# Retention and two feed-forward layers on one core: keeping a second token block in SBUF, splitting inputs earlier, starting the last phase's copies later

## The chip, the cores and the metric

The kernel runs on 1 core of one Trainium2 chip. The metric is the device time of one execution in microseconds (us): 1074.28 us before the change, the median of 3 runs (1074.26 to 1076.01).

## The reference, cut to what matters

Four sequences of 768 tokens with 8 heads of 64 go through a retention layer (a decaying linear attention), and its output, as 3072 rows of 512, through two feed-forward layers of width 2048.

```python
for t in range(S):
    state = gamma[None, :, None, None] * state + np.einsum('bhd,bhe->bhde', k[:, :, t], v[:, :, t])
    y[:, :, t] = scale * np.einsum('bhd,bhde->bhe', q[:, :, t], state)
...
x = np.ascontiguousarray(attn_out.transpose(0, 2, 1, 3)).reshape(B * S, H * D)
h = x @ w_in;  g = np.maximum(0.01 * h, h);               x = g @ w_out     # first layer
h = x @ w_in2; g = h * (1.0 / (1.0 + np.exp(-1.702 * h))); y = g @ w_out2   # second layer
```

## The kernel before, in words

All is computed in float32. A product of two float32 matrices is made of three matmuls on parts: every operand is split into a high part (a rounded copy, made by ScalarE) and a low part (the operand less its high part, a subtraction on VectorE or GpSimd), and high x low, high x high and low x high are added up in PSUM. The weights arrive as float64 words and are turned into float32 in the kernel. The engines' queues are written out by hand: the order of the calls in the code is the order on each engine, and every engine and every queue of transfers takes its instructions strictly in that order. `later.at(n, ...)` puts a step n turns later; a turn is one `later.tick()`, once per tile of the first layer.

**Retention** (`retention`) goes in 24 steps `s`, each a chunk of 128 tokens, 6 chunks a sequence. Tokens are grouped in 6 blocks of 512, so steps 0 to 3 are block 0, steps 4 to 7 block 1. In a step, in this order:

- TensorE makes the scores of chunk s+1 (L277), VectorE masks them (L280);
- from step 4 on a piece n of the first layer's weights is converted (`work_first`): two ScalarE instructions (L172, L173), then four on VectorE (L176, L178, L180, L182), which need the first of ScalarE's;
- TensorE makes the chunk's output: the state's addition (L300, not in the last chunk of a sequence), then L307 and L313, which need the state that VectorE left at L316;
- `a_store` scales the output out of PSUM (VectorE). For block 0 this takes three instructions (L329, which put the two halves of every second head pair in place), then a rounded copy on ScalarE (L338) and the subtraction on GpSimd, so that both parts stay in SBUF, ready as operands. For all other blocks it takes one instruction (L341) and, every second chunk, three transfers into a scratch tensor `xd0[blk]` in HBM (`swapped`, L161 and L163);
- `work_last`: weights piece n-1 is split (ScalarE L154, GpSimd L151) and piece n rounded (L191, on GpSimd for the first two pieces);
- ScalarE scales the keys of chunk s+2 by their decay (L288, 8 instructions);
- SyncE (SP) issues the load of chunk s+4 (L267);
- from step 6 on `ffn_in(0, m)`: one tile of the first layer's first product for block 0, 12 matmuls (L238), and its eviction by ScalarE (L242). Its third matmul needs the low part of weights piece m from GpSimd.

**The first layer's first product for blocks 1 to 5** follows: for each block 16 tiles `m` of 12 matmuls, PSUM in 6 banks, evicted in turn by ScalarE (L242). Beside it ScalarE and VectorE prepare the other weights (`Prep`, 9 pieces a block): a load, conversion three turns later (L172 to L191 and sums), a split one turn after that for some, and a store by SP six turns after the load, in a ring of three places (areas b, b and c). The conversion writes into a place from which the store of three pieces before must have been read.

A block's input comes back from HBM with `x_load` (L205, one transfer of 1 MB on SP's queue into the single buffer `x_raw`) and is split in four quarters with `x_split`, each a ScalarE copy (L154) and a VectorE subtraction (L151). The last quarter's `x_split` also issues the `x_load` of the block after it, which must wait until that quarter has been read. Split inputs lie in two areas in turn: "d" for even blocks, "a" for odd ones.

**The other phases** (L770 and L581 on TensorE) are the remaining three products in Strassen form. The last one (`second2`) is begun in the third's piece 26 by `second2.begin`: its loads at once, and its first four high and low parts (L727 on ScalarE, L151 on VectorE) from 14 turns later on.

Of the kernel before, what the change touches and what calls it, by code (L numbers as in the profile page):

```python
# [24 lines left out]
NP = H // 2  # L25
NC = S // P
KF = DFF // P
TB = 512
NB = NT // TB
CPB = TB // P  # L30
N_STEPS = B * NC

NQ = KF // 2
# [54 lines left out]
def retention_two_ffn(ctx: ExitStack, tc: tile.TileContext, qkv, consts, small, w1i, w1o, w2i, w2o, scratch, out):  # L88
# [30 lines left out]
    def areas(tags, dt=F32):  # L119
        return [Area(t, dt) for t in tags]  # L120
# [9 lines left out]
    later2 = Later()  # L130
# [6 lines left out]

    xs_a = areas("da", F32R)
    xs = [[xs_a[u].view(4 * k, 2, TB) for k in range(NP)] for u in range(2)]
    x0 = xs_a[0].view(0, NP, 2, TB)  # L140
    x_raw = Area("c1").view(0, NP, TB)
    g_area = Area("e")
    g_ring = ring(run_of(g_area, 6, 2), TB)
# [6 lines left out]
    def subtract(o, x, y, e=nc.vector):  # L150
        e.tensor_tensor(out=o, in0=x, in1=y, op=ALU.subtract)  # L151

    def split(hi, lo, src, eng=nc.vector):
        nc.scalar.copy(out=hi, in_=src)  # L154
        subtract(lo, src, hi.bitcast(F32), eng)
# [3 lines left out]
    def swapped(d, s):  # L159

        nc.sync.dma_start(out=d[:, 0::2], in_=s[:, 0::2])  # L161
        for r, t in halves:
            nc.sync.dma_start(out=d[r, 1::2], in_=s[t, 1::2])  # L163

    def load_raw(m):
        raw[m] = t = next(raw_ring).bitcast(U32)
        nc.sync.dma_start(out=t, in_=w1i[m].bitcast(U32).rearrange("p (f two) -> p f two", two=2))
# [36 lines left out]
    def x_load(q):  # L204
        nc.sync.dma_start(out=x_raw, in_=xd0[q])  # L205

    def x_split(q, k):
        split(xs[q % 2][k][:, 0], xs[q % 2][k][:, 1], x_raw[:, k])
        if k == NP - 1 and q + 1 < NB:
            x_load(q + 1)  # L210
# [5 lines left out]
    def work_first(n):  # L216
        if n + 2 < KF:
            load_raw(n + 2)
        if n < KF:
            convert(n)  # L220

    def work_last(n):
        if 0 < n <= KF:
            finish(n - 1)
        if n < KF:
            round_up(*conv[n], nc.gpsimd if n < 2 else nc.vector)
# [19 lines left out]
    def retention():  # L246
# [11 lines left out]
        steps = [(b, c) for b in range(B) for c in range(NC)]  # L258
# [4 lines left out]
        def a_load(s):  # L263
            ins[s] = next(in_ring)
            n = 2 if s < 3 else 4
            for i in range(0, 4, n):
                nc.sync.dma_start(out=ins[s][:, i : i + n], in_=qkv[s, :, i : i + n])  # L267

        def a_scores(s):
            t = ins[s]  # L270
            qT = t[:, 0].rearrange("p (n i) -> p n i", n=NP)
            kT = t[:, 1].rearrange("p (n i) -> p n i", n=NP)
            ps = banks[:, 0:2].rearrange("p e (n i) -> p e n i", n=NP)
            for n in range(NP):
                for e in range(2):
                    r = slice(D * e, D * e + D)
                    nc.tensor.matmul(out=ps[:, e, n], lhsT=kT[r, n], rhs=qT[r, n], start=True, stop=True,  # L277
                                     skip_group_check=True)
            sm = next(sm_ring)
            nc.vector.tensor_tensor(out=sm, in0=ps, in1=mask, op=ALU.mult)  # L280
            sc_t[s] = sm

        def a_decay(s):
            b, c = steps[s]
            if c < NC - 1:
                ks_t[s] = ins[s][:, 2].rearrange("p (h d) -> p h d", h=H)
                for h in range(H):
                    nc.scalar.activation(out=ks_t[s][:, h], in_=ks_t[s][:, h], func=AF.Copy, scale=kdec[:, c, h : h + 1])  # L288
# [31 lines left out]
        def a_store(s, o):  # L320
            blk, cc = divmod(s, CPB)
            cols = slice(cc * P, cc * P + P)
            if cc % 2 == 0:
                a_store.x = next(x_ring)
            x = a_store.x[:, :, cc % 2 * P : cc % 2 * P + P]

            def put(r, u, t):
                n = 2 * P
                nc.vector.tensor_tensor(out=x[r].rearrange("p (m u) i -> p u m i", u=2)[:, u],  # L329
                                        in0=o[t, u, :n].rearrange("p (m i) -> p m i", i=P),  # L330
                                        in1=qdec[t].rearrange("p (m u) i -> p u m i", u=2)[:, u], op=ALU.mult)

            if blk == 0:
                put(slice(0, P), 0, slice(0, P))
                for r, t in halves:
                    put(r, 1, t)

                nc.scalar.copy(out=x0[:, :, 0, cols], in_=x)  # L338
                subtract(x0[:, :, 1, cols], x, x0[:, :, 0, cols].bitcast(F32), nc.gpsimd)
                return  # L340
            nc.vector.tensor_tensor(out=x.rearrange("p (m u) i -> p u m i", u=2),  # L341
                                    in0=o[:, :, : 2 * P].rearrange("p u (m i) -> p u m i", i=P),
                                    in1=qdec.rearrange("p (m u) i -> p u m i", u=2), op=ALU.mult)
            if cc % 2:
                swapped(xd0[blk][:, :, cc * P - P : cc * P + P], a_store.x)
            if s == 2 * CPB + 1:
                x_load(1)

        ins[0] = next(in_ring)
        nc.scalar.dma_start(out=smalls, in_=small)  # L350
# [16 lines left out]
        def keep_warm(n):  # L367

            for _ in range(n):
                nc.tensor.matmul(out=warm, lhsT=idle[:, :P], rhs=idle, start=True, stop=True, skip_group_check=True)  # L370
# [5 lines left out]
        for s in range(len(steps)):  # L376
            if s == 0:
                keep_warm(6)
            elif s + 1 < len(steps):
                a_scores(s + 1)  # L380
            n = None
            if s >= W0 - 2 and done[0] < KF + 1 and (s <= W0 or now_in[s - 1]):
                n = done[0]
                done[0] += 1
                work_first(n)
            o = a_out(s)
            a_store(s, o)
            if n is not None:
                work_last(n)
            if s == 0:  # L390
                a_scores(1)
                keep_warm(6)
            if s + 2 < len(steps):
                a_decay(s + 2)
            if s + 4 < len(steps):
                a_load(s + 4)
            if s in (1, 2):
                load_raw(s - 1)
            if s >= len(steps) - 4:
                x_split(1, s - len(steps) + 4)  # L400
            for m in now_in[s]:
                ffn_in(0, m)

# [95 lines left out]
    def w_split(q, a, b):  # L499
        for hi, lo in w_parts(q, a, b):  # L500
            split(hi.bitcast(F32R), lo.bitcast(F32R), lo)
# [351 lines left out]


    retention()

    h_banks[:] = range(6)
# [14 lines left out]
    for blk in range(1, NB):  # L872
        for m in range(KF):
            n = (blk - 1) * KF + m
            if given < min(N_IN1, (n + 1) * N_IN1 // 64):
                Prep(*names[given], prep_rings).start(later)
                given += 1
            if blk + 1 < NB:
                if m in (8, 9, 10, 11):
                    x_split(blk + 1, m - 8)  # L880
            elif m == 11:
                second1.begin(later, 2 * NQ, 2 * NQ, 3, 1)
            ffn_in(blk, m, second1.place(0, 1, *divmod(m, NQ)) if blk + 1 == NB else None)
            if blk + 1 == NB and m in freed:
                q = freed[m]
                for a, b in ((3, 7), (0, 3)) if m < 11 else ((6, 7), (3, 6), (0, 3)):
                    w_load("1o", q, a, b)
                if m < 11:
                    later.at(3, lambda q=q: w_split(q, 3, 7))
                    later.at(4, lambda q=q: w_split(q, 0, 3))  # L890
            later.tick()
# [14 lines left out]
    def done1(n, blk, i, q):  # L906
# [19 lines left out]
        if i == 2 and q < 3:  # L926
# [8 lines left out]
    second2 = Second({"x": run_of(x_a, 8, 2), "y": run_of(y_a, 8, 2), "z": run_of(z_a, 8, 2),  # L935
                      "ops": run_of(o_a[0], 4, 4) + run_of(o_a[1], 1, 4),
                      "u": run_of(u_a[0], 2, 4) + run_of(u_a[1], 2, 4)},
                     gd2, {"d": (4, 5), "e": (6, 7), "f": (0, 1), "h": (2, 3)})
# [7 lines left out]
    def step2(n):  # L946
        if n < 5:
            w_load("2i", n + 3, 0, 7)
        if 1 <= n <= 5:
            behind.extend(w_steps(n + 2, 3, 7) + w_steps(n + 2, 0, 3))  # L950
        if n in (4, 5):
            todo[n - 4].load()
        if n == 5:
            waiting.extend(todo[2:])
        if 6 <= n < 24 and n % NQ in range(1, 7) and todo:
            p = todo.pop(0)
            behind.extend([lambda: behind.extendleft(reversed(p.steps() + [lambda: p.finish(later2, waiting)]))])
        if n == 26:
            second2.begin(later2, 0, NQ, 4, 14)

    def done2(blk, q):
        if blk < 3:
# [146 lines left out]
```

## Time and profile before

| | |
|---|---|
| median of 3 runs | 1074.28 us (1074.26 to 1076.01) |
| the profiled execution | 1073.59 us |
| its span in the trace | 1071.5 us |
| TensorE (PE) busy | 1052.3 us, 98% |
| VectorE (DVE) busy | 816.0 us, 76% |
| ScalarE (ACT) busy | 585.4 us, 55% |
| GpSimd (POOL) busy | 93.3 us, 9% |

The profiled execution lasts 2.1 us longer than its span and 0.69 us less than the median. Busy shares are means over phases; matmuls overlap, so a busy PE is not PE at its peak. Where PE loses time is read from single stretches.

### The profile page before, as it was taken

The numbers are of one execution on the slowest core, as the hardware profiler recorded it, in microseconds if no ns is written. First come the engines' busy times: TensorE is split into PE (matmuls) and PEld (weight loads), VectorE is DVE, ScalarE is ACT, GpSimd is POOL, SyncE is SP. The second block draws the span as 40 slices with busy tenths as digits, with TensorE's granted clock in tenths as the row PEclk, the third lists the DMA queues.
The fourth block names the chain that finished last, engine by engine and source line by source line (L and its number), as shares of the span: only waits on it lengthen the run. The fifth ranks groups of instructions, "written<-read, shape, count | busy, mean of one in ns | idle before, by whom it ended". The sixth has DMA issues, their size and how long they took to land.

```text
span 1071.5 us, 16963 instructions
## 1 busy us (share of the span) xinstructions
PE 1052.3 (98%) x6042; PEld 902.4 (84%) x6043; DVE 816.0 (76%) x1380; ACT 585.4 (55%) x1116; POOL 93.3 (9%) x91
## 2 busy tenths in 40 slices
PE   8999999999899999999999999999999999999998
PEld 6777788887688888888888999999999788888886
DVE  5988737977796698787788767676867995885883
ACT  5866435645464554544545666465666555555553
POOL 2312100000000000000000104434300000000000
PEclk9999999999999999999999999999999999999999
DMA  9999665998896523525437936648387535335322
GB/s 342 348 396 337 213 228 188 314 316 302 294 350 227 172 80 128 187 79 177 138 123 280 354 121 228 222 157 307 122 316 257 183 99 197 102 96 197 107 70 79
DMA packets 128164, 225.81 MB, mean 211 GB/s; under 512 B 11088, under 2 KB 72784, under 8 KB 124752
## 3 DMA queue, kind: packets, MB, share of 16 engines
q1 hardware_dynamic: 97440, 178.29, 48.7%
q10 hardware_dynamic: 30640, 46.45, 11.7%
q8 instruction: 47, 0.77, 0.3%
q14 instruction: 37, 0.30, 0.1%
HBM read 138.71 MB, written 85.98 MB: 210 GB/s over the span
## 4 chain that ended last, share of the span: by engine, by line
PE 78%; DVE 8%; DMA 8%; ACT 3%; issue 2%; ACTq 0%; SPq 0%; DVEq 0%
PE psum L770 40%; PE psum L581 21%; PE psum L238 12%; DMA h<-qkv 2%; PE psum L277 1%; DMA b<-w1o 1%; PE psum L307 1%; DMA b<-gd 1%; DVE b L151 1%; PE psum L994 1%; DMA wd1o<-b 1%; DVE b L191 1%; DMA xd<-h 1%; PE psum L300 1%; DMA gd<-e 1%
## 5 line engine op out<-in xcount | busy, mean ns | idle before, releaser
L770 PE MATMUL psum<-c,h 128*128 128x512 f32 x1008 | 228.8, 389 | 0.0
L770 PEld LDWEIGHTS psum<-c,h 128*128 128x128 f32 x1008 | 189.2, 188 | 39.3
L770 PE MATMUL psum<-e,h 128*128 128x512 f32 x768 | 182.1, 391 | 1.0 <-DVE e L151 1.0
L770 PEld LDWEIGHTS psum<-e,h 128*128 128x128 f32 x768 | 143.3, 188 | 31.6 <-DVE e L151 1.3
L238 PE MATMUL psum<-d,h 128*128 128x512 f32 x576 | 138.2, 397 | 4.9 <-DVE d L151 3.3
L238 PEld LDWEIGHTS psum<-d,h 128*128 128x128 f32 x576 | 107.8, 190 | 31.1 <-DVE d L151 3.7
L238 PE MATMUL psum<-a,h 128*128 128x512 f32 x576 | 131.5, 389 | 0.0
L238 PEld LDWEIGHTS psum<-a,h 128*128 128x128 f32 x576 | 107.9, 188 | 23.0 <-ACT e L242 0.4
L581 PE MATMUL psum<-b,h 128*128 128x384 f32 x576 | 110.4, 334 | 2.1 <-ACT psum L654 2.1
L581 PE MATMUL psum<-c,h 128*128 128x384 f32 x576 | 110.1, 334 | 0.3 <-DVE d L618 0.3
L581 PEld LDWEIGHTS psum<-b,h 128*128 128x128 f32 x576 | 100.7, 188 | 2.8 <-ACT psum L654 2.8
L581 PEld LDWEIGHTS psum<-c,h 128*128 128x128 f32 x576 | 100.7, 188 | 0.6 <-DVE d L618 0.6
L727 ACT CAST c<-b 128x512 fp32r<-128x512 f32 x96 | 59.2, 622 | 57.1 <-DVE c L151 35.6
L601 ACT ACTIVATE d<-psum 128x384 f32<-128x384 f32 x96 | 47.1, 492 | 65.0 <-PE psum L581 54.8
L151 DVE TENSOR_TENSOR c<-b,c 128x512 fp32r<-128x512 f32 x96 | 65.4, 689 | 18.8 <-ACT c L727 16.6
L242 ACT ACTIVATE e<-psum 128x512 f32<-128x512 f32 x80 | 47.3, 591 | 42.7 <-PE psum L238 37.6
L727 ACT CAST e<-a 128x512 fp32r<-128x512 f32 x77 | 47.3, 622 | 41.6 <-PE psum L770 17.1
L151 DVE TENSOR_TENSOR h<-h 128x384 fp32r<-128x384 f32 (+2 forms) x80 | 44.9, 595 | 31.9 <-ACT h L154 20.4
L151 DVE TENSOR_TENSOR e<-a,e 128x512 fp32r<-128x512 f32 x77 | 52.3, 688 | 18.5 <-ACT e L727 17.1
L151 POOL TENSOR_TENSOR a<-a 128x768 f32<-128x768 f32 x7 | 13.2, 1891 | 509.4 <-DMA h<-wds 461.4
L605 DVE TENSOR_TENSOR d<-psum,d 128x384 f32<-128x384 f32 x96 | 52.1, 549 | 4.3 <-ACT d L601 3.6
L770 PE MATMUL psum<-f,h 128*128 128x512 f32 x192 | 49.0, 390 | 0.0
(148 smaller groups left out, 1469.6 us busy)
## 6 DMA issues: line engine op xcount, KB each, us to landing
gd<-d ACTq DMA_DIRECT2D x128, 192.0 KB, 3.6
h<-qkv SPq DMA_DIRECT2D x21, 1024.0 KB, 8.6
gd<-e ACTq DMA_DIRECT2D x80, 256.0 KB, 5.0
d<-gd SPq DMA_DIRECT2D x64, 256.0 KB, 3.8
b<-gd SPq DMA_DIRECT2D x64, 256.0 KB, 4.0
a<-gd SPq DMA_DIRECT2D x48, 256.0 KB, 5.1
c<-w1i SPq DMA_DIRECT2D x16, 512.0 KB, 7.7
xd<-e SPq DMA_DIRECT2D x12, 512.0 KB, 3.2
```

The lines of the kernel that those rows point to most:

```text
L151: e.tensor_tensor(out=o, in0=x, in1=y, op=ALU.subtract)
L191: e.tensor_tensor(out=f.bitcast(I32), in0=f.bitcast(I32), in1=low.bitcast(I32), op=ALU.add)
L238: nc.tensor.matmul(out=h, lhsT=w[:, a, k], rhs=xs[blk % 2][k][:, c], start=(i == 0), stop=(i == 3 * NP - 1), skip_group_check=True)
L242: nc.scalar.activation(out=t, in_=h, func=AF.Lrelu)
L277: nc.tensor.matmul(out=ps[:, e, n], lhsT=kT[r, n], rhs=qT[r, n], start=True, stop=True, skip_group_check=True)
L300: nc.tensor.matmul(out=kv[r, n], lhsT=ks[:, 2 * n + e], rhs=v[:, n, r], start=(c == 0 and n == 0), stop=True, skip_group_check=True)
L307: nc.tensor.matmul(out=out(n, e), lhsT=v[:, n, r], rhs=sm[:, e, n], start=(n < 2), stop=(c == 0), skip_group_check=True)
L581: nc.tensor.matmul(out=t, lhsT=w[:, k, a], rhs=x[:, b, k], start=(start and m == 0), stop=(m == 5), skip_group_check=True)
L601: nc.scalar.activation(out=s, in_=src, func=AF.Sigmoid, scale=1.702)
L605: nc.vector.tensor_tensor(out=dst, in0=src, in1=s, op=ALU.mult)
L727: nc.scalar.copy(out=t[:, 0], in_=self.block_of(*item))
L770: nc.tensor.matmul(out=t[:, j], lhsT=w[:, j, a], rhs=x[:, b], start=(new and q == 0 and m == 0), stop=(q == NQ - 1 and m == 2), skip_group ...
```

## The change

Three edits. Block 1's retention result now stays in SBUF like block 0's (`blk < 2`), in area "a", so the scratch tensor `xd0[1]`, its load and its `x_split` go; the load of block 2 is issued in step 13. The `x_split` of the next block is called at tiles 2, 4, 6 and 8 instead of 8, 9, 10 and 11. The last phase's first parts are made 22 turns after `second2.begin` instead of 14.

```diff
@@ -137,7 +137,7 @@
     xs = [[xs_a[u].view(4 * k, 2, TB) for k in range(NP)] for u in range(2)]
-    x0 = xs_a[0].view(0, NP, 2, TB)
+    x_first = [t.view(0, NP, 2, TB) for t in xs_a]
@@ -330,7 +330,8 @@
-            if blk == 0:
+            if blk < 2:
+                x0 = x_first[blk]
                 put(slice(0, P), 0, slice(0, P))
                 for r, t in halves:
                     put(r, 1, t)
@@ -343,8 +344,8 @@
-            if s == 2 * CPB + 1:
-                x_load(1)
+            if s == 3 * CPB + 1:
+                x_load(2)
@@ -396,8 +397,6 @@
-            if s >= len(steps) - 4:
-                x_split(1, s - len(steps) + 4)
@@ -876,8 +875,8 @@
             if blk + 1 < NB:
-                if m in (8, 9, 10, 11):
-                    x_split(blk + 1, m - 8)
+                if m in (2, 4, 6, 8):
+                    x_split(blk + 1, m // 2 - 1)
@@ -956,7 +955,7 @@
-            second2.begin(later2, 0, NQ, 4, 14)
+            second2.begin(later2, 0, NQ, 4, 22)
```

Two places show what stands where. ScalarE's queue in steps 4 and 5 of retention, before (L172 and L173 convert a weights piece, L154 splits the one before it, L288 decays the keys; h_84 is the area of the retention chunks, h_412 that of the weights):

```order
L172 ACTIVATE b<-c_233 128x512
L173 ACTIVATE c_233<-c_233 128x512
L288 ACTIVATE h_84<-h_84,f 128x64 x8
L172 ACTIVATE b<-c_233 128x512
L173 ACTIVATE c_233<-c_233 128x512
L154 CAST h_412<-b 128x512
L288 ACTIVATE h_84<-h_84,f 128x64 x8
```

and now, where L339 is the rounded copy that was L338 before (the weights' area is now h_417):

```order
L172 ACTIVATE b<-c_233 128x512
L173 ACTIVATE c_233<-c_233 128x512
L339 CAST a<-h_84 128x4x128
L288 ACTIVATE h_84<-h_84,f 128x64 x8
L172 ACTIVATE b<-c_233 128x512
L173 ACTIVATE c_233<-c_233 128x512
L339 CAST a<-h_84 128x4x128
L154 CAST h_417<-b 128x512
L288 ACTIVATE h_84<-h_84,f 128x64 x8
```

In each of steps 4 to 7 a copy of the chunk's output now stands between the conversion of a weights piece and all that follows on ScalarE; on GpSimd its subtraction likewise stands ahead of the weights piece's.

SP's queue late in block 3, before (L205 is the load of block 5's input, L420 loads of weights, L455 and L456 stores of prepared ones from areas e, f, b and c):

```order
L420 DMA b<-w2i 128x2x256 x2
L455 DMA wds<-e 128x896
L456 DMA wds<-b 128x896
L420 DMA c_1600<-w2i 128x2x256 x2
L205 DMA c_81<-xd_5_71 128x2048
L455 DMA wds<-f 128x896
L456 DMA wds<-c_1600 128x896
```

and now, with every line number below the retention one less:

```order
L419 DMA b<-w2i 128x2x256 x2
L205 DMA c_81<-xd_5_71 128x2048
L454 DMA wds<-e 128x896
L455 DMA wds<-b 128x896
L419 DMA c_1605<-w2i 128x2x256 x2
L454 DMA wds<-f 128x896
L455 DMA wds<-c_1605 128x896
```

The input's load has moved three tiles forward, ahead of one weights load and one pair of stores; it stands in the same way in blocks 1 and 2.

## Rows read from the trace of the kernel before

**Rows 1.** Windows of 20 us: busy time by engine, TensorE clock, DMA share, GB/s
```profile
40.00:60.00 20.00, 20.00 (x237) 15.95 (x235) 18.94 (x28) 13.61 (x38) 5.17 (x4) 1.00 1.02 371
```
**Rows 2.** Chain that ended last, in order of time, blocks 1 to 5: start, length
```profile
134.12 16.56 PE psum L238 x72
...
283.17 76.45 PE psum L238 x336
```
**Rows 3.** Timeline where block 4 begins: start, length, instruction, [idle before <-what ended it]
```profile
266.53 2.34 PE L238 MATMUL psum<-d,h 128*128 128x512 f32 x9 [1.33 <-ACT e L242]
...
272.15 0.33 SPq L205 DMA_DIRECT2D c<-xd  x1
272.18 10.76 PE L238 MATMUL psum<-d,h 128*128 128x512 f32 x39 [3.31 <-DVE d L151]
...
273.01 0.42 SPq L456 DMA_DIRECT2D wds<-c  x1
...
281.40 0.66 ACT L172 ACTIVATE c<-c 128x512 f32<-128x512 f32 x1 [6.21 <-DMA gd<-e]
```
**Rows 4.** Window of 2 us in the same stretch
```profile
274.00:276.00 2.00, 2.00 (x6) 1.53 (x5) 1.79 (x4) 0.73 (x2) 0.00 (x0) 0.50 0.88 303
```
**Rows 5.** Timeline of SP and of ScalarE at the end of block 2
```profile
218.53 0.34 SPq L205 DMA_DIRECT2D c<-xd  x1
...
226.28 0.66 ACT L172 ACTIVATE c<-c 128x512 f32<-128x512 f32 x1 [8.00 <-DMA b<-w1o]
```
**Rows 6.** Timeline of ScalarE in steps 2 to 8 of retention
```profile
20.27 0.62 ACT L338 CAST d<-h 128x512 fp32r<-128x512 f32 x1 [0.64 <-DVE h L329]
20.80 2.01 ACT L288 ACTIVATE h<-h,f 128x64 f32<-128x64 f32 x8
...
24.22 0.69 ACT L172 ACTIVATE b<-c 128x512 f32<-128x512 f32 x1
...
36.48 1.28 ACT L242 ACT_TABLE_LOAD   x1
...
42.93 0.57 ACT L242 ACTIVATE e<-psum 128x512 f32<-128x512 f32 x1
...
43.96 0.70 ACT L172 ACTIVATE b<-c 128x512 f32<-128x512 f32 x1 [0.46 <-ACT e L242]
```
**Rows 7.** Timeline of VectorE in the same steps
```profile
18.94 1.29 DVE L329 TENSOR_TENSOR h<-psum,f 128x256 f32<-128x256 f32 x3 [0.30 <-PE psum L313]
...
24.94 1.02 DVE L176 TENSOR_SCALAR c<-c 128x512 uint32<-128x512 uint32 x1
...
27.39 0.42 DVE L316 TENSOR_TENSOR b<-psum,f 128x256 f32<-128x256 f32 x1
27.73 0.68 DVE L341 TENSOR_TENSOR h<-psum,f 128x512 f32<-128x512 f32 x1
...
39.64 0.42 DVE L176 TENSOR_SCALAR c<-c 128x512 uint32<-128x512 uint32 x1
```
**Rows 8.** Timeline of GpSimd in step 2
```profile
20.97 1.27 POOL L151 TENSOR_TENSOR d<-h,d 128x512 fp32r<-128x512 f32 x1 [1.91 <-ACT d L338]
```
**Rows 9.** Timeline of TensorE in steps 6 to 9
```profile
33.33 3.02 PE L238 MATMUL psum<-d,h 128*128 128x512 f32 x12
...
39.62 3.01 PE L238 MATMUL psum<-d,h 128*128 128x512 f32 x12
...
45.75 3.04 PE L238 MATMUL psum<-d,h 128*128 128x512 f32 x12
...
49.80 0.69 PE L300 MATMUL psum<-h 128*64 128x64 f32 x16
```
**Rows 10.** Timeline of TensorE in step 12
```profile
67.30 1.16 PE L277 MATMUL psum<-h 64*128 64x128 f32 x16 [0.54 <-DMA h<-qkv]
```
**Rows 11.** Timeline of ScalarE and TensorE in the third product, behind `second2.begin`
```profile
793.42 0.62 ACT L504 CAST h<-h 128x512 fp32r<-128x512 f32 x1 [3.08 <-DMA h<-wd2o]
...
795.38 2.37 PE L581 MATMUL psum<-b,h 128*128 128x384 f32 x12 [1.47 <-ACT psum L654]
```

## The prediction

> **What bounds the kernel now.** I read the busy shares first: TensorE 98% of the span. Then the chain that ended last, to see whether any other engine holds a long piece of it: it runs through TensorE's product L238 for hundreds of matmuls at a time [rows 2]. Then windows, which say where the remaining 2% lie. Even in retention, where the change works, TensorE is busy for 20.00 of 20.00 us while transfers move 371 GB/s [rows 1]. So shorter work elsewhere gains nothing by itself; a gain must remove a wait of TensorE, and a loss is a new wait of TensorE that nothing behind it gives back, since all behind it is TensorE's own work. Last I read timelines where the three edits act.
>
> **Part 1, the splits at tiles 2, 4, 6, 8: a gain of 7.1 us.** The row of 336 matmuls in 76.45 us gives 0.2275 us a matmul at full speed [rows 2]. The chain has its two L238 rows at 134.12 and 283.17 with 960 matmuls in blocks 1 to 5, so between these starts lie 624 matmuls in 149.05 us; at 0.2275 they would take 142.0. Lost there: 7.1 us.
>
> Where it goes is seen at block 4's start [rows 3]: TensorE waits 1.33 us for ScalarE's eviction, then 3.31 us for VectorE's L151, the last quarter of that block's split. SP's L205, the load of the block after, gets off at 272.15, when that split ends. The load stood at the head of SP's queue, with the stores (L456) of prepared weights behind it. These land late, the conversions that reuse their places start late (ScalarE's L172 stood idle 6.21 us ahead of 281.40; 8.00 us at the same place of block 2, where L205 went at 218.53 [rows 5]), and behind them stand ScalarE's evictions. So the late split delays the load, the load the stores, the stores the evictions, these TensorE and the next split. The remaining 2.5 us (7.1 − 1.33 − 3.31) I put down to the clock: just behind the 3.31 us wait it is granted at 0.50, the 1.2 GHz level, and 2 us hold 6 matmuls [rows 4].
>
> After the change the last quarter comes at tile 8 instead of 11, three tiles earlier: 3 × 12 × 0.2275 = 8.2 us, as much as the longest of the ScalarE waits. I expect the waits and the slow clock to go: −7.1. The upper end is 0, if ScalarE's queue stays late for another reason. Block 1's own split at steps 20 to 23 vanishes; it lies beside TensorE's work, so 0.
>
> **Part 2, block 1 kept in SBUF: a loss of 11.1 us.** What it takes away, three transfers for each of two chunk pairs and one load, 2.1 MB in all, lies beside a busy TensorE [rows 1]: 0. What it adds in each of steps 4 to 7 is two more L329 instead of one L341 on VectorE, a copy on ScalarE and a subtraction on GpSimd, 0.6 to 1.3 us each. What matters is their place. The copy L339 waits for VectorE's L329, these stand behind VectorE's words of weights piece n, which need ScalarE's L172; and behind the copy stand ScalarE's L154, the decays, the eviction and the next L172. ScalarE and VectorE, which ran freely past each other, now wait for each other once a step. The round, from rows of before:
> - L172 to VectorE's L316: 27.39 − 24.22 = 3.17 [rows 6, 7]. L176 took 1.02 there and 0.42 at 39.64 [rows 7]; with the short one the stretch is 2.57.
> - L316 to the store: 27.73 − 27.39 = 0.34 [rows 7].
> - three L329 to the copy: 20.27 − 18.94 = 1.33; copy to the next on ScalarE 0.53, and eight L288 2.01 [rows 6, 7].
> - L154, taken like the copy: 0.53. L242 to the next L172: 43.96 − 42.93 = 1.03 [rows 6].
> - copy to GpSimd's start 0.70, and 1.27 an operation there, twice (copy's and weights') [rows 6, 8].
>
> 2.57 + 0.34 + 1.33 + 0.53 + 0.53 + 2.01 + 1.03 = 8.3 us, while TensorE's tiles of these steps follow each other in 6.29 and 6.13 us [rows 9]. So the round, not TensorE, sets the pace of steps 4 to 8:
> - Step 4: L316 as before at 27.39, stores 27.73, copy 29.06, decays 29.59, next L172 at 31.60.
> - Step 5 (last chunk of a sequence, no L316): stores 34.17, copy 35.50, decays 36.56 to 38.57; GpSimd's two subtractions 36.20 to 38.74. Tile 0's third matmul needs the second of them: 38.8 instead of 33.8 [rows 9], +5.0.
> - Step 6: L172 at 38.74 (GpSimd must have read its place). GpSimd still rounds piece 1, so 3.17: L316 41.91, stores 42.25, copy 43.58, GpSimd to 46.82, third matmul of tile 1 at 46.9 instead of 40.1, +6.8. Decays to 46.65, the table load, 1.28 [rows 6], then L242 and L172 at 48.96.
> - Step 7: L316 51.53, copy 53.20, GpSimd to 56.44, tile 2's third matmul 56.5 instead of 46.2, +10.3. Next L172 57.30.
> - Step 8, block 2, without the copy: L316 at 60.47 (3.17 taken), and L300 of the next chunk, which needs it, at 60.85 instead of 49.80 [rows 9]: +11.05.
>
> From there all is as before and TensorE bound; nothing is given back. With 2.57 everywhere it is 9.9, with 3.17 everywhere 12.3. I take 11.1.
>
> The short and the long L176 differ by whether GpSimd works at the time. The Trainium skill (SBUF — State Buffer, "Who interferes with whom") states a rule for it: VectorE in its two-port mode and GpSimd lock each other out for a whole instruction, whoever comes first. The rows agree where they show 1.02 beside 0.42; by the rule alone, with GpSimd busier in every step, the sum would take 12.3 for 11.1.
>
> TensorE's first new wait is some 5 us, longer than the 3.31 us after which the clock was at 0.50 [rows 3, 4]. No row shows what that costs here; below 0 (the tiles wait again anyway), above 2.5 (the remainder of part 1). I take 1.0, near the low end, since the round holds the pace whatever TensorE's clock.
>
> The load of block 2 moves to step 13, ahead of a chunk's load on SP. At the same place before, in step 9, TensorE waited 0.54 us for a chunk [rows 10]. In step 13 the same at a new place: 0; bounds −0.5 (no wait) and +3.0 (a tile of 3.02 us [rows 9] less as cover in step 14).
>
> **Part 3, copies 22 turns ahead: 0.** TensorE's wait of 1.47 us at 795.38 comes from ScalarE's eviction, and that from ScalarE's 3.08 us wait at 793.42 for a weights transfer, ahead of the moved copies [rows 11]. The wait isn't theirs, before or after. Bounds ±1.5, a wait of this size removed or added.
>
> **Sum.** The profiled execution lasts 1073.59 (span 1071.5 and 2.1 around it): + 11.1 + 1.0 − 7.1 + 0 + 0 = 1078.6. The median of the runs is 0.69 above it: **1079.3 us**.
>
> **Rivals.** 0.2%, 2.15 us, is about what a measurement of this kernel tells from no change.
>
> *The round is hidden* (other side: faster). If the copy finds its input done, because VectorE gets its stores ahead early enough, a round would be at most the 6.15 us of a tile's pitch and TensorE would not wait. Against it: the parts add up to 8.3, all measured, and queues are strictly in order. It decides below 6.15. Then 1074.28 − 7.1 = 1067.2.
>
> *Transfers are the bound.* 371 GB/s while all engines are busy [rows 1] might mean that TensorE's work there is paced by loads. Then 2.1 MB less would give 2.1/371 × 1000 = 5.7 us and hide the round: 1067.2 − 5.7 = 1061.5. Against it: no wait for a transfer over 0.54 us on TensorE.
>
> *The clock falls in each of the four waits*, not once: three times 1.0 to 2.5 more, 1082.3 to 1086.8. For it: 0.50 after 3.31 us [rows 4]. The Trainium skill (TensorE: Matmul & The Clock Gate, "What's actually happening") says that a monitor sets the clock by how busy TensorE has been of late, which would speak for this rival. The trace of before agrees by the 0.50, and shows no run of waits like these.
>
> *The splits bring nothing.* ScalarE is late by conversions and stores in themselves, 6 us after the load is gone; the split then waits at tile 8 as it did at 11. For it: ScalarE's wait at 281.40 [rows 3] names a transfer of the first product's output, not a weights store. 1079.3 + 7.1 = 1086.4.
>
> **How the numbers follow.** Forecast 0.72; hidden round 0.09; transfers 0.03; clock each time 0.06; splits idle 0.10. The forecast's own range is 1076 to 1083 (part 2 ±1.2, clock −1.0 to +1.5, the load to +3.0, part 3 ±1.5, not all at one end); 0.05 of its chance lies within 0.2%. The whole range takes in the two slower rivals and stops short of the faster ones: 1074 to 1087. Faster 0.12 (the two faster rivals), same 0.05, slower 0.83.
>
> **What the profile would show.** ScalarE's new copies start near 29, 35.5, 43.6 and 53.2; the third matmuls of tiles 0 to 2 come 5, 7 and 10 us late, with GpSimd named; block 1's first tile starts near 146 instead of 134.1. In blocks 2 to 4 the 3.31 us wait on VectorE, the 8.00 and 6.21 us waits of ScalarE and the 0.50 clock are gone, and L204, as the load is then numbered, leaves without a stop. The third product's 1.47 us wait stands. Wrong would be: block 1 starting near 134 (the round hidden), or block 5 later than its start plus part 2 (splits idle).

## The result, and the profile after

The changed kernel takes 1082.4 us (median of 5 runs, 1079.61 to 1083.4) against 1074.28 before. By the means of the five runs on each side it is 0.66% slower, ratio 1.0066 with a 95% interval of 1.0048 to 1.0083 (the two medians alone give 0.76%). 1079.3 had been forecast. The profiled execution lasts 1082.14, its span 1080.4, 8.9 us longer than before.

Where it went is read from the chain that ended last, set against [rows 2] (start, length, what):

```profile
147.54 13.84 PE psum L238 x60
...
287.04 81.89 PE psum L238 x360
368.94 32.64 PE psum L769 x144
```

Block 1 starts 147.54 − 134.12 = 13.4 us later. The first product ends at 368.9; before it ended at 283.17 + 76.45 = 359.6, so only 9.3 us are left there: blocks 1 to 4 give 4.1 back. From there to the end 0.4 us more comes back.

ScalarE in steps 4 to 8 (against [rows 6]; L339 is the new copy, which also serves block 0):

```profile
29.48 0.62 ACT L339 CAST a<-h 128x512 fp32r<-128x512 f32 x1 [3.56 <-DVE h L329]
...
35.82 0.62 ACT L339 CAST a<-h 128x512 fp32r<-128x512 f32 x1 [2.64 <-DVE h L329]
...
43.65 0.62 ACT L339 CAST a<-h 128x512 fp32r<-128x512 f32 x1 [3.35 <-DVE h L329]
...
46.73 1.28 ACT L242 ACT_TABLE_LOAD   x1
...
53.30 0.62 ACT L339 CAST a<-h 128x512 fp32r<-128x512 f32 x1 [2.97 <-DVE h L329]
...
57.30 0.66 ACT L172 ACTIVATE b<-c 128x512 f32<-128x512 f32 x1 [0.46 <-ACT e L242]
```

This is the round: every copy stops ScalarE for some 3 us, each time for L329. VectorE in turn waits 1.9 to 3.5 us a step for ScalarE's L172, as here in step 7:

```profile
49.78 0.43 DVE L176 TENSOR_SCALAR c<-c 128x512 uint32<-128x512 uint32 x1 [3.47 <-ACT b L172]
```

TensorE beside it (against [rows 9, 10]):

```profile
37.02 0.96 PE L238 MATMUL psum<-d,h 128*128 128x512 f32 x2 [3.61 <-ACT h L154]
39.08 4.63 PE L238 MATMUL psum<-d,h 128*128 128x512 f32 x10 [1.11 <-POOL h L151]
...
48.68 3.01 PE L238 MATMUL psum<-d,h 128*128 128x512 f32 x12 [1.55 <-ACT e L242]
...
56.89 4.61 PE L238 MATMUL psum<-d,h 128*128 128x512 f32 x12 [2.02 <-ACT e L242]
...
62.52 0.68 PE L300 MATMUL psum<-h 128*64 128x64 f32 x16
...
96.89 0.69 PE L300 MATMUL psum<-h 128*64 128x64 f32 x16 [1.48 <-DVE b L316]
...
103.92 1.16 PE L277 MATMUL psum<-h 64*128 64x128 f32 x16 [1.93 <-DMA h<-qkv]
```

Tiles 0 to 2 come late, and two of them are slow besides: 4.63 us for ten matmuls, 4.61 for twelve, where [rows 9] have 3.02. The windows around these two tiles (columns as in [rows 1]) show a granted clock of 0.50, the 1.2 GHz level, and of 0.72 in the mean:

```profile
38.00:44.00 6.00, 4.92 (x12) 3.50 (x14) 4.11 (x9) 2.48 (x7) 2.28 (x2) 0.50 0.46 173
...
56.00:62.00 6.00, 5.11 (x22) 3.78 (x24) 3.94 (x7) 4.96 (x15) 1.76 (x2) 0.72 0.75 242
```

Where blocks 3 and 4 meet (against [rows 3, 5]), TensorE's wait for the split is gone, but two waits for ScalarE's evictions are left:

```profile
279.42 5.73 PE L238 MATMUL psum<-d,h 128*128 128x512 f32 x24 [0.78 <-ACT e L242]
287.04 13.21 PE L238 MATMUL psum<-d,h 128*128 128x512 f32 x57 [1.89 <-ACT e L242]
```

and ScalarE, at the end of block 2, still stands behind a store:

```profile
234.82 0.66 ACT L172 ACTIVATE b<-b 128x512 f32<-128x512 f32 x1 [6.96 <-DMA wd1o<-b]
```

In the third product (against [rows 11]) all is as it was:

```profile
802.78 0.62 ACT L503 CAST h<-h 128x512 fp32r<-128x512 f32 x1 [3.16 <-DMA h<-wd2o]
...
804.75 2.35 PE L580 MATMUL psum<-b,h 128*128 128x384 f32 x12 [1.55 <-ACT psum L653]
```

### The profile page after: what moved, and what is told of

It reads as the page before. It is cut to its first block, busy times and chain, and to the rows that moved or that the text cites. A ratio compares the mean times of both kernels' runs of the same rounds, so it can differ in the third digit from the quotient of the medians.

```text
span 1080.4 us, 16965 instructions
## 1 busy us (share of the span) xinstructions
PE 1054.2 (98%) x6042; PEld 904.0 (84%) x6043; DVE 813.2 (75%) x1384; ACT 585.4 (54%) x1116; POOL 97.9 (9%) x95
## 4 chain that ended last, share of the span: by engine, by line
PE 78%; DVE 8%; DMA 7%; ACT 4%; issue 2%; ACTq 1%; SPq 0%; POOL 0%; DVEq 0%
PE psum L769 40%; PE psum L580 20%; PE psum L238 13%; PE psum L277 2%; DMA wd1o<-b 1%; PE psum L307 1%; DMA h<-wd2o 1%; PE psum L993 1%; DMA h<-qkv 1%; PE psum L313 1%; PE psum L300 1%; ACT e L242 1%; DMA c<-w2i 1%; ACT b L172 1%; DVE h L329 1%
## 5 line engine op out<-in xcount | busy, mean ns | idle before, releaser
L238 PE MATMUL psum<-d,h 128*128 128x512 f32 x576 | 140.4, 402 | 11.0 <-ACT e L242 6.2
```

The costliest lines, as they stand in the source:

```text
L238: nc.tensor.matmul(out=h, lhsT=w[:, a, k], rhs=xs[blk % 2][k][:, c], start=(i == 0), stop=(i == 3 * NP - 1), skip_group_check=True)
```

## Experiments

Runs of one kernel spread by 0.6 to 8.5 us here (the kernel before went from 1072.81 to 1079.48 in 29 runs). So beside the ratio of each run to the kernel before, which goes by all runs and can lie 1 us off what the two medians give, the start of block 1 and TensorE's waits are taken from its profile. One profile isn't exact either: in the six whose retention is that of the kernel before (its own, e1_splits, e3_later, e7_prep, e8_hol, e12_prep_alone) block 1 starts between 134.1 and 136.0, so a difference of less than 2 us there isn't told from none. Two theories stand at the start: the loss is the round that the copy closes between ScalarE and VectorE, or it is the added work, the clock or the moved load. For the splits: the load at the head of SP's queue made ScalarE late, or something else did.

**The three parts alone.** The earlier splits (e1_splits), block 1's stay in SBUF (e2_kept), and the later start of the last phase (e3_later), each on the kernel before:

```diff
# e1_splits
-                if m in (8, 9, 10, 11):
-                    x_split(blk + 1, m - 8)
+                if m in (2, 4, 6, 8):
+                    x_split(blk + 1, m // 2 - 1)
# e2_kept
-            if blk == 0:
+            if blk < 2:
+                x0 = x_first[blk]
...
-            if s == 2 * CPB + 1:
-                x_load(1)
+            if s == 3 * CPB + 1:
+                x_load(2)
...
-            if s >= len(steps) - 4:
-                x_split(1, s - len(steps) + 4)
# e3_later
-            second2.begin(later2, 0, NQ, 4, 14)
+            second2.begin(later2, 0, NQ, 4, 22)
```

Expected of the splits: 

> The kernel before with the earlier splits alone (tiles 2, 4, 6, 8). By the trace of the changed kernel TensorE takes 144.95 us from the first tile of block 1 to 336 matmuls before the end of block 5, before it was 149.05: the splits give back 4.1 us and two waits of 0.78 and 1.89 us stay. Theory (the splits are worth 4.1 wherever they stand): 1074.3 - 4.1 = 1070.2, block 1's first tile at 134.1. Rival (block 1's stay in SBUF is what lets the splits gain, since it spares a load): little of it here, 1072.5 to 1074.3. Rival (my sum of the prediction): 1067.2.

Measured: 1070.91 us beside 1074.85 for the kernel before, ratio 0.9954 (0.9940 to 0.9967). TensorE's waits are those of the changed kernel, 0.78 and 1.89 us. Block 1 starts at 136.0 instead of the 134.1 that I gave, within the spread. The splits are worth 3.9 us by the medians without the rest, 4.9 by the ratio (3.5 to 6.4); my 7.1 is refuted.

Expected of block 1's stay: 

> Block 1 kept in SBUF alone, splits and last phase as before. Theory (a round between ScalarE and VectorE, 11.1 us, plus TensorE's clock, plus a wait for a chunk's load): block 1's first tile at 147.5 instead of 134.1, and 1074.3 + 13.4 = 1087.7. Rival (the loss is dearer because it meets the late splits, or is partly paid back by the load of block 2 that is there earlier): block 1 at 147.5 all the same, but the time 2 us or more off 1087.7.

Measured: 1085.51 beside 1074.85, ratio 1.0093 (1.0074 to 1.0111); block 1's first tile at 147.7. The whole loss is this part's, 10.7 us by the medians and 10.0 by the ratio, 2 us or more less than the trace of the changed kernel let expect. By the letter that meets the rival's condition; but the run that was profiled took 1088.31, the longest of the six, and the times don't settle it.

Expected of the later start: 

> The last phase's first parts begun 22 turns ahead instead of 14, alone. Theory: 1074.3 - 0.3, not told from no change (1073.5 to 1074.8), the 1.47 us wait of TensorE in the third product still there. Rival (the copies lie in the way of something): off by 1 us or more either way.

Measured: 1074.68 beside 1074.85, ratio 0.9997 (0.9985 to 1.0009); the wait is 1.15 us. It does nothing that can be told.

**The round broken (e4_defer).** The changed kernel, with block 1's copy and subtraction called one step later:

```diff
-                nc.scalar.copy(out=x0[:, :, 0, cols], in_=x)
-                subtract(x0[:, :, 1, cols], x, x0[:, :, 0, cols].bitcast(F32), nc.gpsimd)
+                def parts():
+                    nc.scalar.copy(out=x0[:, :, 0, cols], in_=x)
+                    subtract(x0[:, :, 1, cols], x, x0[:, :, 0, cols].bitcast(F32), nc.gpsimd)
+
+                if blk == 0:
+                    parts()
+                else:
+                    kept.append(parts)
                 return
...
                 work_first(n)
+            while kept:
+                kept.pop(0)()
             o = a_out(s)
```

> The changed kernel with one edit: in steps 4 to 7 the copy on ScalarE and the subtraction on GpSimd of a chunk are called one step later, behind the conversion of the next weights piece, so that the copy finds its input done; all instructions are the same. Theory (the loss is the round that the copy closes): ScalarE no longer waits for L329, tiles 0 to 2 start near 33.3, 39.6, 45.8, TensorE's clock stays at 1.00, and what is left is VectorE's 0.6 us more a step in steps 4 to 7 at most, 0 to 2.4 us, and the 1.9 us wait for a chunk's load: block 1's first tile at 134 to 139, time 1069 to 1074. Rival (the added work itself, on VectorE or GpSimd, or the moved load is the loss): block 1 near 147, time near 1082.

Measured: 1076.17 beside 1074.85, ratio 1.0009 (0.9995 to 1.0023); block 1's first tile at 139.85, not 147.54. ScalarE's timeline:

```profile
29.99 0.62 ACT L340 CAST a<-h 128x512 fp32r<-128x512 f32 x1
...
36.08 0.62 ACT L340 CAST a<-h 128x512 fp32r<-128x512 f32 x1 [1.42 <-DVE h L329]
...
42.66 0.60 ACT L340 CAST a<-h 128x512 fp32r<-128x512 f32 x1
```

Only one copy of the four still waits (the fourth, at 50.20, doesn't), and the same instructions in another order take 6 us less. But block 1's start lies beyond the 134 to 139 that I gave and the time beyond 1069 to 1074. Tile 0 is nearly on time at 33.85, tiles 1 and 2 are not, at 44.92 and 51.06, since TensorE has a wait of a new kind, behind which its clock falls again (0.91 in the mean from 40 to 60; L307 takes 1.95 us for 1.05):

```profile
41.41 1.12 PE L300 MATMUL psum<-h 128*64 128x64 f32 x16 [2.89 <-DVE b L316]
42.29 1.95 PE L307 MATMUL psum<-b,h 128*64 128x128 f32 x16
```

So VectorE is late next, and by more than its two added instructions, 0.6 us a step.

**What still holds VectorE: the load, the rounding, GpSimd.** Three edits tell these apart. First the load of block 2 moved from step 13 to step 19 (e5_load), then on top of that the rounding of two more weights pieces on GpSimd (e6_round):

```diff
# e5_load, on e4_defer
-            if s == 3 * CPB + 1:
+            if s == 5 * CPB - 1:
                 x_load(2)
# e6_round, on e5_load
-            round_up(*conv[n], nc.gpsimd if n < 2 else nc.vector)
+            round_up(*conv[n], nc.gpsimd if n < 4 else nc.vector)
```

> The run with the deferred copy (e4_defer), and the load of block 2 issued in step 19 instead of 13. In e4_defer block 1's first tile started at 139.8 and TensorE waited 1.38 and 1.59 us in the two steps behind that load, the second time for a chunk. Theory (the 1 MB load in step 13 delays the chunks' loads): both waits go, block 1 near 137, time 3 us under e4_defer's, 1073 where the kernel before is at 1074.5. Rival (transfers are late there anyway, as in the kernel before, where TensorE idled 2.6 us between 60 and 90): waits of the same size stay, less than 1 us gained.

> As e5_load, and the rounding of weights pieces 2 and 3 moved from VectorE to GpSimd, as that of pieces 0 and 1 already is: some 0.7 us of VectorE less in steps 6 and 7, 1.3 us of GpSimd more. In e4_defer VectorE was busy 19.64 of 20 us from 40 to 60, and TensorE's 2.89 us wait in step 6 was for its L316. Theory (with the round gone VectorE is what is late next): 0.5 to 1.5 us under e5_load. Rival (GpSimd's longer stretches slow VectorE's 0.42 us instructions to 1.02, or GpSimd becomes late for the tiles): equal or up to 2 us over e5_load.

Measured, beside 1074.97 for the kernel before: 1075.39, ratio 0.9997 (0.9985 to 1.0010), block 1 at 139.3; and 1074.65, ratio 0.9995 (0.9983 to 1.0008), block 1 at 138.5. The 2.89 us wait is in both. The load brings 0.5 us, not 3: as the rival had it, waits of 0.76 and 1.51 us are left at 88.01 and 90.67. The rounding brings 0.8, within what I gave. Both are less than profiles differ by, and the times don't tell the two apart either.

Then block 1's subtractions taken from GpSimd: left out, with a copy on ScalarE in their place (e9_nosub), or made by VectorE itself (e10_dve):

```diff
# e9_nosub, on e5_load
-                    subtract(x0[:, :, 1, cols], x, x0[:, :, 0, cols].bitcast(F32), nc.gpsimd)
+                    if blk == 0:
+                        subtract(x0[:, :, 1, cols], x, x0[:, :, 0, cols].bitcast(F32), nc.gpsimd)
+                    else:
+                        nc.scalar.copy(out=x0[:, :, 1, cols], in_=x)
# e10_dve, on e5_load
-                    subtract(x0[:, :, 1, cols], x, x0[:, :, 0, cols].bitcast(F32), nc.gpsimd)
+                    subtract(x0[:, :, 1, cols], x, x0[:, :, 0, cols].bitcast(F32), nc.gpsimd if blk == 0 else nc.vector)
```

> As e5_load, but the four subtractions of block 1 in steps 5 to 8 leave GpSimd: in their place ScalarE writes a second copy, so the low parts of block 1's input are not the reference's and the run only tells times. In e5_load block 1's first tile starts at 139.3 although the round is gone, and VectorE's L178 took 1.49 to 1.53 us in steps 5 to 8 instead of 0.41 while GpSimd's subtractions of block 1 ran. Theory (GpSimd holds VectorE up, about 1.1 us a subtraction, and VectorE is what is late): VectorE's L176 and L178 fall back to 0.42 in part, TensorE's 2.89 us wait for L316 shrinks by 1 to 2.5 us, block 1's first tile at 136 to 138. Rival (the two more L329 a step, 0.6 us each, are the rest): block 1 stays within 0.7 us of 139.3.

> As e5_load, but VectorE itself makes block 1's four subtractions, 0.68 us each. Theory (each costs VectorE about 1.1 us already where it stands on GpSimd): block 1's first tile up to 1.7 us earlier than e5_load's 139.3, or equal, since the subtraction also stands ahead of L316 now. Rival (they cost VectorE nothing on GpSimd): 4 x 0.68 = 2.7 us later, 141 to 142.

Measured: without the subtractions block 1 starts at 134.92, 4.4 us earlier than in e5_load and more than I gave; 1070.36 beside 1075.32, ratio 0.9959 (0.9943 to 0.9975). TensorE's wait for L316 is 1.81 instead of 2.89 us:

```profile
39.59 0.69 PE L300 MATMUL psum<-h 128*64 128x64 f32 x16 [1.81 <-DVE b L316]
```

In e5_load this L300 stands at 41.64. So of the 4.4 us 2.05 are VectorE's lateness there; 1.4 more are TensorE's clock, which falls behind the longer wait only (tile 1 follows at 45.14 and 41.67; the clock from 40 to 60 is 0.91 in the mean, and 1.00 without the subtractions), and the rest are waits further on.

With the four subtractions on VectorE block 1 starts at 137.9; 1074.95 beside 1075.32, ratio 0.9994 (0.9984 to 1.0003). The 1.4 us to e5_load are within the spread of profiles, so which engine should make them isn't told. But the rival's 141 to 142 is out: four instructions of 0.68 us more on VectorE don't make it later than GpSimd's beside it do. The two timelines of e5_load show how GpSimd holds VectorE up, VectorE's first, then GpSimd's:

```profile
31.28 1.19 DVE L176 TENSOR_SCALAR c<-c 128x512 uint32<-128x512 uint32 x1
32.38 1.50 DVE L178 TENSOR_SCALAR b<-b 128x512 f32<-128x512 f32 x1
33.91 0.43 DVE L180 TENSOR_SCALAR b<-b 128x512 uint32<-128x512 uint32 x1
```

```profile
30.90 1.27 POOL L151 TENSOR_TENSOR a<-h,a 128x512 fp32r<-128x512 f32 x1 [0.90 <-ACT a L340]
32.14 1.46 POOL L151 TENSOR_TENSOR h<-b,h 128x512 fp32r<-128x512 f32 x1
```

GpSimd's operations end at 32.17 and 33.60; L176 ends 0.30 behind the first, L178 0.28 behind the second. In e9_nosub the same two take what they take alone, and L180 is held up, by the one subtraction that GpSimd has left in this step (the weights piece's, 31.55 to 32.83):

```profile
30.95 0.45 DVE L176 TENSOR_SCALAR c<-c 128x512 uint32<-128x512 uint32 x1
31.28 0.42 DVE L178 TENSOR_SCALAR b<-b 128x512 f32<-128x512 f32 x1
31.73 1.38 DVE L180 TENSOR_SCALAR b<-b 128x512 uint32<-128x512 uint32 x1
```

**SP's queue freed (e8_hol).** The kernel before, with the loads of blocks 3 to 5 taken from behind the split:

```diff
-        if k == NP - 1 and q + 1 < NB:
+        if k == NP - 1 and q == 1:
             x_load(q + 1)
...
+                if blk > 1 and m == 3:
+                    x_load(blk + 1)
                 if m in (8, 9, 10, 11):
```

> The kernel before with the splits at tiles 8 to 11 as they were, and only the loads of blocks 3 to 5 taken from behind the last quarter's split and issued at tile 3 of the next block, where nothing holds them: SP's queue no longer stands still behind a load. Theory (the load at the head of SP's queue, and the stores behind it, made ScalarE late): ScalarE's 8.00 and 6.21 us waits shrink, the 3.31 us wait of TensorE for the split too, 2 to 4 us under the kernel before. Rival (the place of the splits in ScalarE's and VectorE's queues does it): the 3.31 us wait stays, the time within 1 us of the kernel before.

Measured: 1073.58 beside 1074.97, ratio 0.9985 (0.9973 to 0.9997), which lies between what the theory and what the rival gave. The load of block 4 now goes at 239.14, ahead of stores that follow at once, and ScalarE's 8.00 and 6.21 us waits are gone: from 215 to 295 none is over 3.5 us (earlier in block 2 there is one of 5.66, for a weights load). TensorE waits as before:

```profile
266.70 2.36 PE L238 MATMUL psum<-d,h 128*128 128x512 f32 x9 [1.04 <-ACT e L242]
272.39 43.36 PE L238 MATMUL psum<-d,h 128*128 128x512 f32 x183 [3.33 <-DVE d L151]
```

The theory of my prediction falls: the blocked queue made ScalarE's longest waits, but hardly TensorE's, and freeing it brings 1.4 of the 7.1 us by the medians.

**The round of the weights pieces (e7_prep, e12_prep_alone).** What made ScalarE late instead is seen in e1_splits, where it splits the prepared weights:

```profile
245.04 0.94 ACT L154 CAST e<-c 128x896 fp32r<-128x896 f32 x1 [3.34 <-DVE c L151]
...
252.11 0.94 ACT L154 CAST f<-b 128x896 fp32r<-128x896 f32 x1 [2.90 <-DVE b L151]
...
259.19 0.94 ACT L154 CAST e<-b 128x896 fp32r<-128x896 f32 x1 [2.90 <-DVE b L151]
```

The split of a piece waits for VectorE's sums, these wait for ScalarE's L172 of the same piece, and an eviction, often a quarter of the input's split and the next L172 stand behind the split: a round like retention's, 7.07 us a piece (5.91 to 7.07 in block 3 of the kernel before), while a piece is due every 1.78 tiles of 2.73 us, 4.85. One edit, on e1_splits (e7_prep) and on the kernel before (e12_prep_alone), calls the split one turn later, and with it the store of what it makes:

```diff
-                clock.at(4, self.split if split else self.keep)
+                clock.at(5, self.split if split else self.keep)
-                clock.at(6, self.store_split if split else self.store)
+                clock.at(7 if split else 6, self.store_split if split else self.store)
```

> The earlier splits alone (e1_splits), and the split of a prepared weights piece one turn later, its store too. In blocks 1 and 3 ScalarE waits some 2.9 us once per piece for VectorE's sums, a round of 7.07 us per piece while 1.78 tiles of 2.72 us are 4.84: the evictions fall behind to 12.3 us, and TensorE still loses 2.9 us at the end of block 3. Theory (the same kind of round as in retention, and a second eviction inside it shortens it): ScalarE's waits shrink, the evictions stay less than 10 us behind, TensorE's waits there go: up to 2.9 us under e1_splits, 1067.5 to 1069 where e1_splits is at 1070.9. Rival (VectorE's own work per piece, 5.6 us, keeps the pace, or the later store holds back the next conversion): within 1 us of e1_splits or over it.

> The kernel before with the split of a prepared weights piece one turn later (its store too), as in e7_prep, and the input splits left at tiles 8 to 11. Theory (TensorE's waits in blocks 3 and 4 come from the round of 7.07 us a piece, which makes ScalarE late for the evictions and for the input's split alike): without the round the late splits are on time too, the 3.31 us wait for the split is gone or under 1 us, and the time comes within 2 us of e7_prep's 1068.1. Rival (the place of the splits matters by itself): the wait for the split stays near 3 us, and the time is 1071 to 1074.

Measured: 1068.09 beside 1074.97, ratio 0.9933 (0.9916 to 0.9950), and 1068.53 beside 1075.62, ratio 0.9940 (0.9923 to 0.9958), both as their theories had it. In e7_prep TensorE goes through blocks 1 to 5 with no wait, each in 192 × 0.2275 us:

```profile
134.93 43.82 PE L238 MATMUL psum<-a,h 128*128 128x512 f32 x192
178.59 43.68 PE L238 MATMUL psum<-d,h 128*128 128x512 f32 x192
222.10 43.68 PE L238 MATMUL psum<-a,h 128*128 128x512 f32 x192
```

In e12_prep_alone, with the splits where they were before, the 3.31 us wait is gone as well; one of 0.54 is left, although ScalarE stands for 7.07 us behind a store:

```profile
276.34 32.94 PE L238 MATMUL psum<-d,h 128*128 128x512 f32 x144 [0.54 <-ACT e L242]
```

```profile
274.59 0.66 ACT L172 ACTIVATE c<-c 128x512 f32<-128x512 f32 x1 [7.07 <-DMA wds<-c]
```

So the lost 7 us were the weights pieces' round, and moving the input splits only eases what it leaves behind. The round isn't opened, though, but shortened: in e7_prep the split still waits for VectorE's sums, and two pieces follow each other in 5.91 us.

```profile
244.31 0.94 ACT L154 CAST f<-b 128x896 fp32r<-128x896 f32 x1 [2.32 <-DVE b L151]
...
250.22 0.94 ACT L154 CAST e<-b 128x896 fp32r<-128x896 f32 x1 [1.83 <-DVE b L151]
```

The evictions and the input's splits now stand in what was ScalarE's wait, and the next L172 comes right behind the split. That TensorE no longer waits is measured; why 5.91 is short enough where 4.85 is the pace wasn't taken apart, nor were the split and the store tried each by itself.

**The best of both (e11_best).** On e7_prep, which keeps only block 0 in SBUF, the load of block 1 moved from step 9 to step 17, and the last phase begun 22 turns ahead:

```diff
-            if s == 2 * CPB + 1:
+            if s == 4 * CPB + 1:
                 x_load(1)
...
-            second2.begin(later2, 0, NQ, 4, 14)
+            second2.begin(later2, 0, NQ, 4, 22)
```

> The fastest so far (e7_prep: the earlier splits, the weights' splits one turn later), and two edits that should help or cost nothing: the load of block 1 moved from step 9 to step 17, and the last phase's copies 22 turns ahead. In e7_prep TensorE waited 1.36 us for a chunk at 68.12, some 10 us behind that load's issue at 57.77, and 1.95 us at 86.33 for L316. Theory: the first wait goes, perhaps the second, 1 to 3 us under e7_prep, 1065 to 1067. Rival (the load is as much in the way in step 17, or comes too late for block 1's split in step 20): equal or slower than e7_prep.

Measured: 1065.69 us (1065.55 to 1066.18) beside 1075.32, ratio 0.9908 (0.9895 to 0.9920): faster than both kernels. Block 1 starts at 133.0, TensorE's wait for a chunk at 68 is gone (the later start of the last phase did nothing by itself, e3_later), and the window over blocks 1 to 5 is full:

```profile
140.00:360.00 220.00, 220.00 (x973) 182.15 (x972) 165.68 (x347) 119.29 (x205) 0.00 (x0) 1.00 0.82 284
```

## Why the prediction held, and where its steps failed

The forecast of the profiled execution was 1078.6; it took 1082.14. The 3.5 us between are 1.3 in retention, 3.0 in the splits, and −0.8 in the later phases and around the span. By the number alone the rival with the clock falling in each wait, 1082.3 to 1086.8, would fit 1082.4 as well as the forecast's own range does; the traces tell them apart.

**The round, 11.1 us: right in mechanism, and 11.5 in size.** The copies were forecast at 29.06, 35.50, 43.58 and 53.20 and started at 29.48, 35.82, 43.65 and 53.30; the L172 behind the round was forecast and found at 57.30. L316 in step 8, forecast at 60.47, came 0.4 us later:

```profile
60.86 0.41 DVE L316 TENSOR_TENSOR b<-psum,f 128x256 f32<-128x256 f32 x1
```

It ended at 61.27, and from there L300 could have started, 11.5 us later than at 49.80. That the order of the calls makes most of the loss, and not the amount of work, is shown by e4_defer, where block 1 starts 7.7 us earlier; what is left there is told below. What I had wrong in it is who holds tiles 1 and 2: the profile names ScalarE's eviction of the tile before, which the round delays too, not GpSimd's low part.

**The clock, 1.0 us: 1.25.** I argued that the round holds the pace whatever TensorE's clock. That is so for tile 0, which ended at 43.71 while its eviction, behind the copy, the decays and the table load, came at 48.02. But tile 2 is the last behind the round: it took 4.61 instead of 3.02, and L277 and L300 follow it without a gap, at 62.52, while L316 had ended at 61.27. So 1.25 of the tile's 1.6 us are lost, and TensorE was 12.7 us late there, not 11.05 + 1.0. The rival with the clock falling in each wait is half right: it fell in the first and third, not in tile 1, which began after a wait of 1.55 us and took 3.01; and of the two falls one cost nothing.

**The load of block 2, 0: nearly.** From that L300 to block 1 it is 85.0 us, before 84.3 (134.12 − 49.80). The chunk's wait grew from 0.54 to 1.93, others shrank. e5_load puts the place of the load at 0.5 us; neither is more than profiles differ by.

**The transfers taken away, 0: right.** e9_nosub has them gone, and the round and the subtractions too, and starts block 1 where kernels with the retention of before do, not 5.7 us earlier; the rival that took them for the bound falls. What I held against it was misread: TensorE did wait longer than 0.54 us for a transfer before, ahead of the first tile: 1.47 us at 26.98 and 0.98 at 30.75.

```profile
26.98 1.16 PE L277 MATMUL psum<-h 64*128 64x128 f32 x16 [1.47 <-DMA h<-qkv]
```

**The splits, −7.1: the step that failed.** "The late split delays the load, the load the stores, the stores the evictions" was a chain read off the named releasers, and e8_hol cuts it without moving TensorE's 3.3 us wait. In the changed kernel too the load of block 5 held SP's queue for only 2.6 us, up to 273.59, where it had been 7.6, and the waits didn't all go. The loss that I had worked out, 7.1 us, was right and is all to be had (e12_prep_alone: 7.1 by the medians, 6.5 by the ratio), but its cause is the round of the weights pieces, which the earlier splits leave in place: 4.1 in the trace, 3.9 alone by the medians. The rival that they bring nothing because ScalarE is late by itself named the right engine; by size 3.0 of the 7.1 us were its.

**The last phase, 0: right,** by the same wait in the same place, and by e3_later.

**Not foreseen:** what lies under the round. I priced GpSimd's subtraction by its own time and by 0.6 us in L176. With the round open, GpSimd's four subtractions cost block 1's start 4.4 us, by VectorE's lateness and the clock that falls in the wait for it (e9_nosub). So keeping block 1 did not pay in a better order either: e5_load, e6_round and e10_dve, with the earlier splits in them, come out level with the kernel before, and the earlier splits alone 3.9 us under it.

## What to carry to other kernels

Before putting an instruction on an in-order queue, follow its input back: if that lies behind work that itself waits for something earlier on this queue, the two engines take turns, and the sum of the round's durations is to be held against the pace of the engine that should be the bound; calling the same instruction one step later opened one round here (e4_defer) and shortened the other from 7.07 to 5.91 us (e7_prep). A wait of many microseconds on an engine is no loss until the engine that sets the time waits for it, and the releaser that the profile names there is a lead, to be cut by an experiment before a sum rests on it. Work given to an idle engine is not free when it slows the busy one.

## What the runs showed of the hardware

A GpSimd operation of 1.3 to 1.5 us held up VectorE's L176, L178 and L180 almost to its end: 1.19, 1.50 and 1.38 us instead of 0.45, 0.42 and 0.43, each ending some 0.3 us behind GpSimd's. The Trainium skill (SBUF — State Buffer, "Who interferes with whom") has a rule for VectorE in its two-port mode and GpSimd: whoever comes first holds the shared ports for a whole instruction. The rows above agree with the lock; in which mode these instructions ran no row shows. In the prediction I had priced it at 0.6 us in two of the steps, from the one row with 1.02.

TensorE's clock was granted at 0.50 after a wait of 3.61 us and stayed there through a tile of 4.63 us; it fell again around a wait of 2.02 us and did not around one of 1.55. e2_kept shows the same, 0.50 and 0.72 in the same two windows. The first cost 2.1 us in its tile (4.63 for ten matmuls, which take 2.5 at the pace of 3.02 for twelve), the second 1.6, and only of the second did something, 1.25 us, reach the end.
